# Scores of a linear-attention head in three blocks of 64x64, with sums moved onto TensorE by identity products, and a new written order of the attention stage

## The chip, the cores and the metric

The kernel runs on one core of a Trainium2 chip. The metric is the device time of one execution in microseconds, the median over the runs shown. Engines are named as the profile names them: PE is TensorE's matmul, PEld its weight load, DVE VectorE, ACT ScalarE, POOL GpSimd, SP the queue that issues the transfers.

## The reference

Three stages follow each other. The first is a recurrence with a decaying state for 2 batches of 8 heads (768 steps, 48 wide); its result, 1536 tokens of 384 numbers, goes through two feed-forward layers.

```python
def _attn_ref(r, k, v, w, u) -> np.ndarray:
    ...
    for t in range(S):
        kt, vt, rt, wt = (k[:, :, t], v[:, :, t], r[:, :, t], w[:, :, t])
        cur = np.einsum('bhd,bhe->bhde', u[None] * kt, vt)
        y[:, :, t] = np.einsum('bhd,bhde->bhe', rt, state + cur)
        state = wt[:, :, :, None] * state + np.einsum('bhd,bhe->bhde', kt, vt)

def _moe_ref(x, w_in, w_out) -> np.ndarray:      # 384 -> 2048 -> 384
    h = x @ w_in
    g = np.where(h > 0.0, h, alpha * (np.exp(np.minimum(h, 0.0)) - 1.0))
    return (g @ w_out).astype(np.float32)

def _moe2_ref(x, domain_probs, w1, w2):          # 4 experts, 384 -> 1024 -> 384
    p = domain_probs / (domain_probs.sum(-1, keepdims=True) + 1e-09)
    for e in range(E):
        h = np.maximum(x @ w1[e], 0.0)
        out += p[:, e:e + 1] * (h @ w2[e])
```

## The kernel before

**Attention.** The 768 steps are cut into chunks of 128, six to a batch, so there are 12 chunks, taken in the order SEQ: the two batches alternate, and chunks 0 and 1 of the program are the first of each batch. The 8 heads lie as 4 pairs (p) of two (j): head j of a pair has its 48 rows at partitions 64j to 64j+47. A chunk passes through these steps (name of the token, function, what it does):

- `iw`, `ik`, `lv` load decays, k and r, and v (three buffers each); `su` and `pr` are two scans over the decays on DVE, `kd` and `rd` multiply k and r by them, `g` (own) multiplies r by k.
- `tr` transposes `kd` on PE; `pa` (scores) makes for each head the 128x128 products of its keys and queries; `ow` (own_scores) sums the own products of a step with `ublock`.
- `am` (masked) keeps of the scores what lies above the diagonal, either in one DVE multiplication by `mask` or as an ACT copy and a POOL select.
- `vo` multiplies own scores by v on DVE (tile `bv`); `pp` (update) makes the chunk's part of the state, `us` (updated) adds it to the aged state on DVE, `ws` ages the state.
- `py` (values) sums in two PSUM banks the state's part and the part of the masked scores; `ys` (results) adds both banks to `bv` on DVE; `xs` (parts) splits the sum into a rounded high part and the rest, which the feed-forward products read; `xd` spreads them by a transfer.

**Feed-forward 1.** Its weights come in 32 pieces; `wl` loads one, `wa`, `wb` and `wc` (rest) make its high and low parts. `h` is a hidden block (9 products of 128x128 by 512), `e` and `el` its activation and low part, `z` the second layer (9 products), `dr` takes the sums.

**Order.** Nothing is scheduled: each engine executes its instructions in the order in which the list `ORDER` of such tokens calls the steps; a letter at the end of a token names the engine (A, D, P). A token `n2` adds two products of the tile `idle` (L136) ahead of the next use of a bank: they compute nothing that is used. The first hidden block needs the `x` of four chunks. The list's part up to `|` holds the attention and the first 16 hidden blocks; the experts follow, and there PE runs without a gap.

**Products.** The attention's operands are float32; the profile shows two PE instructions for each such product, and one for each product of the rounded type (fp32r) that the feed-forward layers use. Products whose rows and columns of the array differ (partitions 0 to 63 or 64 to 127 on either side) can stand beside each other.

Of the kernel before, what the change touches and what calls it, by code (L numbers as in the profile page):

```python
# [26 lines left out]
LEAD = 3  # L27
WN = NPAIR * (LEAD + C)
# [46 lines left out]
wl4 wa4D iw1 iw0 su1 ik1 wl0 pr1 ik0 wb4P ik3 kd1P su0 rd1P n2 pa1 tr1A wa0D iw3 pr0 wl2 g1D lv1 rd0D iw5 n2 ow1 kd0P  # L75
n1 pp1 su3 g0D am1S py1 kd3D vo1 wb0P iw2 tr3A lv0 tr0A ik2 g3P pr3 rd3P pa0 lv2 am0S ys1 wl1 lv3 su2 us1 ow0 pp0 py0
pr2 xs1P ws3A wc0P ik4 us0 iw4 vo0 xd1 ow3 wa1D rd2D wa2D lv4 pp3 pa3 am3D wb1P wb2P vo3 n5 py3 su4 ys0 ws2A ys3 wl16
kd2P ik5 wc1P g2P pa2 xs0P lv5 tr2A pr4 ow2 am2M py2 kd4P rd4P iw6 vo2 xd0 wl3 su5 n2 pa4 xs3D ys2 us3 kd5P g4D pp2
pr5 ow4 xs2P ik6 ws5A rd5P am4D g5P us2 xd3 vo4 tr4A wc2P su6 n2 pa5 ow5 vo5 xd2 ws4A iw7 am5M wa16D tr5A wl5 pp4
kd6P wa3D py5 lv6 pr6 py4 wc4P tr6A wb3P ys5 lv7 pp5 rd6D wb16D pa6 wc3P us4 ik7 su7 wl7 us5 wc16P xs5P ws6A am6D h2  # L80
wl17 wa5D iw8 h0 kd7D ys4 e2 wl18 g6P pr7 tr7A ws7A pp6 el2D wb5D h1 wa17D e0 ow6 vo6 us6 ik8 g7P wc5P e1 xd5 wa18D
el0D h3 wb17D rd7P iw9 pp7 wl19 us7 py6 ys6 pa7 wb18P xs6P lv8 el1D wc17D am7M h13 z0 ik9 su8 wa19D ow7 iw11 ws8A
wa7D vo7 xd6 z1 e3 wc18P kd8P py7 tr8A su9 lv9 wl6 wb19P z2 pp8 e13 ys7 wl20 wb7P el3D wc19D pr8 xs7D wl21 rd8D xs4D
wc7D xd7 wl23 h12 wa6D kd9P pa8 z3 g8P e12 wb6P us8 am8D g9D el12D tr9A py8 wc6D xd4 dr3A ow8 wa20D wa21D h15 wb20D
pr9 ik10 vo8 el13P rd9P ws9A lv10 h14 pp9 wl22 e15 ow9 iw10 ys8 wb21D vo9 us9 wa22D pa9 am9D wc20P el15D xs8D h4
wa23D z12 wc21P py9 e14 z13 ik11 su10 wb22P e4 wc22D su11 el14P wb23P kd10P lv11 pr10 h5 el4P rd10P h7 z14 ys9 wc23P
e5 pa10 el5D ws10A am10S h6 kd11P g10D ow10 pr11 vo10 z15 e6 dr15D z4 xs9P py10 g11D xd8 z5 el6D ys10 e7 ow11 rd11D
vo11 pa11 xs10D z6 am11D el7P ws11A py11 ys11 xs11P h16 xd9 e16 h17 xd10 el16P h18 z7 e17 dr7A e18 el17P h19 el18P
z16 xd11 | h8 z17 e19 e8 el8P el19D h9 h10 z18 e9 z8 e10 el9D el10D h11 z9 e11 el11D z10 wl24 wl25 wa25D wa24D h20
z11 wb24P wb25P e20 dr11A z19 h21 wl8 wl10 wc25P dr19D wa8D e21 el20P h22 wl9 wc24P wb8D z20 el21D wa9D e22 wc8P  # L90
wa10D wb9D h23 wl11 z21 wc9P el22D wl26 e23 h24 wb10D wa26D el23D e24 wl12 z22 h25 wc10D wa11D wb26P e25 el24P wb11D
z23 wl14 el25D h28 wc11D wl28 h26 dr23D wa12D wc26D e26 z24 el26D wl27 h27 z25 wb12P e28 wa27D e27 wa28D el28D h29
z26 wb27D el27D wc12P e29 wl29 h31 wc27P wb28D el29D z28 wl13 wa14D e31 wb14P wc28P z27 dr27D h30 wa29D el31P e30
wl15 h32 wa15D z29 el30D wb29P wa13D h35 e32 wc14P el32D z30 wl31 e35 wb13D h33 wa31D wc13P z31 wb15P e33 el35D dr31D
h36 el33P wl30 z32 wa30D h34 wb30P wc29P e36 z33 e34 el34D h37 el36D wc30D h38 wc15D z34 e37 wb31P z36 e38 el38P h39
el37D z35 z37 wc31D dr35D e39 el39P h40 h41 e40 z38 el40P h42 e42 z39 e41 dr39D el41D h43 el42D z40 e43 el43D h44 z41
e44 h45 el44P z42 e45 h46 el45P z43 e46 el46P h47 dr43D z44 e47 z45 z46 el47D z47 dr47D
# [4 lines left out]
def kernel_body(ctx, tc, wkr, vv, uu, w_in, w_out, w1, w2, dp, out):  # L102
# [52 lines left out]
    for t, limit in zip(limits, (1.0, 1 / DOWN)):  # L155
# [106 lines left out]
    def attn(i):  # L262
# [71 lines left out]
        def masked(e):  # L334

            for j in range(2):
                am = tile_of(f"am{j}", 2)
                if e == "D" or (e == "M" and j == 0):
                    mul("D", am, b["pa"][j], mask.unsqueeze(1).to_broadcast([P, NPAIR, C]))
                else:  # L340
                    copy("A", am, b["pa"][j])
                    nc.gpsimd.affine_select(out=am, in_=am, pattern=[[0, NPAIR], [1, C]], compare_op=ALU.is_gt, fill=0.0,
                                            base=0, channel_multiplier=-1)
                free()
# [11 lines left out]
        def update():  # L356
            b["pp"] = pp = bank()[:, :NPAIR * D].rearrange("q (p d) -> q p d", p=NPAIR)
            for p in range(NPAIR):
                for j in range(2):
                    h = 2 * p + j  # L360
                    nc.tensor.matmul(pp[64 * j:64 * j + 64, p, :], lhsT=b["kdt"][:, p, 64 * j:64 * j + 64],
                                     rhs=b["vs"][:, D * h:D * h + D], start=True, stop=True)

        def updated():
            if first:
# [4 lines left out]

        def values():
            b["py"] = py = half_banks()
            if not first:
                for q in range(2):
                    for p, j, o in QUARTERS[q]:
                        nc.tensor.matmul(py[p & 1][64 * o:64 * o + 64, q], lhsT=aged[64 * j:64 * j + D, D * p:D * p + 64],
                                         rhs=b["rd"][64 * j:64 * j + D, p], start=q == 0, stop=False, skip_group_check=True)
# [6 lines left out]
        def results():  # L384
# [4 lines left out]
        def parts(e):  # L389
            split(i, b["bv"], e)  # L390
# [3 lines left out]
                "pp": update, "py": values, "xs": parts, "xd": lambda: spread(i)}  # L394
# [4 lines left out]
    def step(n):  # L399
# [24 lines left out]
        def elu_lo(e):  # L424
            sub(e, b["t"][:, 1], b["e"], b["t"][:, 0])
# [28 lines left out]
    def do(order):  # L454
        for token in order:
# [3 lines left out]
            name, n, e = re.fullmatch(r"([a-z]+)(\d+)([ADMPS]?)", token).groups()  # L459
# [433 lines left out]
def laid_out(i):  # L893
# [17 lines left out]
    vv = np.zeros((P, NCH, 912), np.float32)  # L911
# [3 lines left out]
    vv[:, :, 512:512 + DM] = np.asarray(i["v"]).reshape(2, 8, 6, C, D).transpose(3, 0, 2, 1, 4).reshape(P, NCH, DM)  # L915
    u = np.zeros((2, 64, 4), np.float32)
# [30 lines left out]
```

## Time and profile before

| | |
|---|---|
| median of 3 runs | 650.49 us (650.23 to 650.81) |
| time of the profiled execution | 652.48 us |
| its span, first to last instruction | 650.7 us |
| PE busy | 634.5 us (98%), 3454 instructions |
| DVE busy | 500.2 us (77%), 726 instructions |
| POOL, ACT busy | 358.7 us (55%), 301.8 us (46%) |
| chain of work that ended last | PE 84%, DVE 9%, DMA 3% |

Busy shares are means over the whole span; the stages differ, so the rows below are read by stage. An instruction's own time on PE includes its flight through the array; how fast instructions follow each other is read from the starts of neighbouring groups.

### The profile page before, as it was taken

To read this page: it belongs to the slowest core of one execution; us is meant where nothing else is said; L and a number is where in the kernel's file an instruction comes from. 1 tells how busy PE (TensorE), PEld (TensorE's weight loads), DVE (VectorE), ACT (ScalarE), POOL (GpSimd) and SP (SyncE) were. 2 spreads that over 40 slices of the span, in tenths; PEclk is the share of its full clock that TensorE was granted. 3 is DMA by queue.
4 is the path that set the end of the run, shared out by engine and by line. 5 is a ranking of instruction groups with operands and counts; after the bars stand their busy time and mean duration, and the time that the engine had idled before them with its cause. 6 is when DMAs were issued, how large, how long until landed. Compare 5 with 4: busy or idle time off the path is not lost.

```text
span 650.7 us, 9404 instructions
## 1 busy us (share of the span) xinstructions
PE 634.5 (98%) x3454; PEld 516.1 (79%) x3454; DVE 500.2 (77%) x726; ACT 301.8 (46%) x581; POOL 358.7 (55%) x320
## 2 busy tenths in 40 slices
PE   8898999999999999999999999999999999999995
PEld 6676777788888788888888888888888888888884
DVE  7889998723788854499786886987977968967683
ACT  2437666364766556548353434424443433344230
POOL 5775625231324236546553775876876876854252
PEclk9799999999999999999999999999999999999999
DMA  8747570040322400001212122103121121400012
GB/s 319 246 149 250 186 215 16 13 154 1 95 75 73 131 18 1 0 1 37 103 42 73 34 73 91 25 16 107 41 62 61 42 73 34 123 1 1 0 49 103
DMA packets 20971, 50.94 MB, mean 78 GB/s; under 512 B 2680, under 2 KB 3880, under 8 KB 20916
## 3 DMA queue, kind: packets, MB, share of 16 engines
q1 hardware_dynamic: 20772, 50.25, 23.9%
q8 instruction: 29, 0.48, 0.3%
q14 instruction: 26, 0.21, 0.1%
q10 hardware_dynamic: 144, 0.00, 0.0%
HBM read 46.68 MB, written 2.38 MB: 75 GB/s over the span
## 4 chain that ended last, share of the span: by engine, by line
PE 84%; DVE 9%; DMA 3%; POOL 1%; issue 1%; SPq 0%; ACT 0%; DVEq 0%; POOLq 0%
PE second L666 28%; PE bank L433 13%; PE bank L412 12%; PE chain_a L605 9%; PE chain_b L605 6%; PE chain_p L637 4%; PE chain_c L605 3%; PE chain_d L605 3%; PE chain_e L605 1%; PE bank L323 1%; DMA raw<-in_w_in 1%; DMA kr<-in_wkr 1%; DVE hl L182 1%; DVE raw L219 1%; PE bank L381 1%
## 5 line engine op out<-in xcount | busy, mean ns | idle before, releaser
L666 PE MATMUL second<-hl,w2s 128*128 128x512 f32 x864 | 230.8, 389 | 0.1
L666 PEld LDWEIGHTS second<-hl,w2s 128*128 128x128 f32 x864 | 162.0, 188 | 34.4 <-DVE hl L182 0.5
L684 POOL TENSOR_TENSOR x<-scaled,x 128x512 f32<-128x512 f32 x60 | 84.2, 1424 | 91.5 <-DVE scaled L676 91.3
L412 PE MATMUL bank<-x,w 128*128 128x512 f32 x432 | 105.3, 392 | 0.5 <-DVE e L420 0.5
L433 PE MATMUL bank<-hl,w 128*128 128x512 f32 x432 | 105.1, 391 | 0.0
L659 DVE SCALAR_TENSOR_TENSOR hl<-terms,hl 128x512 fp32r<-128x512 f32 x92 | 96.0, 1055 | 10.6 <-ACT hl L653 10.6
L412 PEld LDWEIGHTS bank<-x,w 128*128 128x128 f32 x432 | 80.3, 188 | 18.4 <-DVE e L420 0.9
L433 PEld LDWEIGHTS bank<-hl,w 128*128 128x128 f32 x432 | 80.5, 188 | 17.6 <-issue 0.7
L182 POOL TENSOR_TENSOR sums<-blocks,sums 128x512 fp32r<-128x512 f32 (+1 forms) x56 | 74.8, 1344 | 28.4 <-ACT sums L186 26.2
L523 POOL TENSOR_TENSOR blocks<-blocks 128x256 f32<-128x256 f32 x84 | 72.6, 883 | 1.1 <-DMA blocks<-in_w 0.4
L420 DVE SCALAR_TENSOR_TENSOR e<-e,bank 128x512 f32<-128x512 f32 x48 | 32.6, 682 | 44.7 <-ACT e L416 43.5
L620 ACT ACTIVATE terms<-chain_b 128x512 f32<-128x512 f32 x28 | 16.7, 598 | 106.0 <-PE chain_b L605 106.0
L653 ACT ACTIVATE hl<-terms 128x512 fp32r<-128x512 f32 x96 | 58.2, 624 | 14.1 <-PE second L666 6.8
L620 ACT ACTIVATE terms<-chain_a 128x512 f32<-128x512 f32 x28 | 16.7, 598 | 77.7 <-PE chain_a L605 77.7
L224 POOL TENSOR_TENSOR raw<-raw,t 128x384 int32<-128x384 int32 x20 | 22.0, 1100 | 51.7 <-ACT t L220 39.3
L605 PE MATMUL chain_a<-x,sums 128*128 128x512 f32 x168 | 47.3, 390 | 0.0
L415 ACT ACTIVATE e<-bank 128x512 f32<-128x512 f32 x48 | 28.4, 593 | 36.8 <-PE bank L412 28.9
L182 POOL TENSOR_TENSOR hl<-e,hl 128x512 fp32r<-128x512 f32 x18 | 23.4, 1297 | 36.6 <-ACT hl L186 36.6
L676 DVE TENSOR_TENSOR scaled<-second,pr 128x512 f32<-128x512 f32 x60 | 40.5, 686 | 3.0 <-PE second L666 1.8
L186 ACT ACTIVATE hl<-e 128x512 fp32r<-128x512 f32 x48 | 30.0, 628 | 24.5 <-DVE e L420 16.7
L617 DVE TENSOR_TENSOR terms<-terms,chain_a 128x512 f32<-128x512 f32 x42 | 28.7, 683 | 14.2 <-PE chain_a L605 13.6
L182 POOL TENSOR_TENSOR w<-raw,w 128x384 fp32r<-128x384 f32 x21 | 22.4, 1070 | 27.6 <-ACT w L186 27.6
(116 smaller groups left out, 1001.0 us busy)
## 6 DMA issues: line engine op xcount, KB each, us to landing
raw<-in_w_in SPq DMA_DIRECT2D x16, 384.0 KB, 3.4
kr<-in_wkr SPq DMA_DIRECT2D x12, 512.0 KB, 6.0
raw<-in_w_out SPq DMA_DIRECT2D x16, 384.0 KB, 3.6
blocks<-in_w SPq DMA_DIRECT2D x16, 384.0 KB, 3.3
raw<-in_w SPq DMA_DIRECT2D x16, 384.0 KB, 4.3
v<-in_vv SPq DMA_DIRECT2D x12, 456.0 KB, 4.7
w<-in_wkr SPq DMA_DIRECT2D x12, 262.5 KB, 4.3
gw<-in_wkr SPq DMA_DIRECT2D x12, 262.0 KB, 2.7
```

What stands on the lines that cost most here:

```text
L182: engines[e].tensor_tensor(o, a, b.bitcast(F32), ALU.subtract)
L412: nc.tensor.matmul(ph, lhsT=wi[:, sa, f, kk, :], rhs=x[:, kk, c0:c0 + nch, sm], start=(kk == 0 and i == 0), stop=(kk == 2 and i == 2))
L420: nc.vector.scalar_tensor_tensor(b["e"], b["e"], -1.0, b["ph"], ALU.add, ALU.max)
L433: nc.tensor.matmul(pxs[q, bl][d][:, :cols], lhsT=wo[:, sa, f, d * P:(d + 1) * P], rhs=b["t"][:, sm], start=(f == 0 and i == 0), stop=(f == ...
L523: nc.gpsimd.tensor_tensor(*(places(blocks[u], p) for p in (r, a, c)), ALU.subtract if op == "-" else ALU.add)
L605: nc.tensor.matmul(banks[c], lhsT=weights(u, r, sa), rhs=tokens(r)[:, sm], start=r in HEADS and i == 0, stop=i == 2, skip_group_check=True)
L620: nc.scalar.activation(out=new({0: 0, 6: 5, 3: 2, 5: 3, 8: 4}[r]), in_=ps, func=AF.Copy, scale=-1.0 if r in (6, 8) else 1.0)
L653: nc.scalar.activation(out=hls[f, b][:, 0], in_=results[f, b], func=AF.Copy if weighted else AF.Relu)
L659: nc.vector.scalar_tensor_tensor(hls[f, b][:, 1], results[f, b], 0.0, hls[f, b][:, 0].bitcast(F32), ALU.max, ALU.subtract)
L666: nc.tensor.matmul(sums[d], lhsT=w[:, sa, f, d * P:(d + 1) * P], rhs=hls[4 * h + f, b][:, sm], start=f == i == 0, stop=f == 3 and i == 2)
L676: nc.vector.tensor_tensor(o, sums[d], prs[h // 2, b], ALU.mult)
L684: nc.gpsimd.tensor_tensor(x2[:, d, s], scaled[d], x2[:, d, s], ALU.add)
```

## The change

Seven edits, all in the attention stage and the weights of feed-forward 1:

1. **Scores** (`pa`): of the four 64x64 blocks of a head's scores the one that the mask clears entirely is no longer made. First keys meet all 128 queries (16 instructions of 64 columns in the array by 128), second keys the last 64 (16 instructions by 64). Neighbouring pairs use opposite halves of the columns. Each head's scores are 384 wide over 4 pairs instead of 512, and `mask` has the same shape, so `am` is always one multiplication of 128x384 for each j.
2. **Values**: the masked part is made in two sets of 16 instructions by 64 columns, second queries over all 128 keys, first queries over 64 keys. For that v is loaded in another layout, 1088 wide instead of 912. The state's part becomes a step of its own, `pq`.
3. **ys with E** (chunks 0 to 4): `bv` is added in PSUM by two products with the identity, in place of two DVE sums.
4. **xs with E** (chunks 0 to 4): ACT copies the high part from PSUM, two products with `minus` (the negated identity) subtract it there, ACT copies the rest out. Before, one ACT copy and one DVE or POOL subtraction.
5. **us with E** (chunks 0 to 3): the aged state is added by an identity product (not for chunks 0 and 1, which have none), and ACT copies the sum.
6. **wc with E** (5 pieces): the low part of a weight piece is made by two products and an ACT copy.
7. **ORDER** is new. Tokens by count up to `|`: `am` 12 on DVE (before 6 on DVE, 3 on both ways, 3 on ACT and POOL), `g` on DVE 1 (6), `rd` on DVE 3 (5), `xs` on DVE 0 (5). Of the `idle` products 11 + 1 are left (13 + 12).

```diff
+wl16 wa16D wl0 iw0 iw1 ik0 wa0D ik1 wl4 su0 wb16P wc16E wb0P kd0P iw2 pr0 rd0P wc0E lv0 su1 pa0 wl17 tr0A wa4D iw5
...
+        def rest(e):
...
+            if e == "E":
+                t = bank()[:, 0:DM]
+                difference(t, hi, wt64[key][:, 0, s])
+                copy("A", lo, t)
+                free()
...
+    def difference(t, a, hi):
+        nc.tensor.matmul(t, lhsT=ident, rhs=a, start=True, stop=False)
+        nc.tensor.matmul(t, lhsT=minus, rhs=hi, start=False, stop=True)
...
         def scores():
-            b["pa"] = pa = [heads_bank() for _ in range(2)]
-            for p in range(NPAIR):
-                for j in range(2):
-                    nc.tensor.matmul(pa[j][:, p, :], lhsT=b["kd"][64 * j:64 * j + D, p, :],
-                                     rhs=b["rd"][64 * j:64 * j + D, p, :], start=True, stop=True)
+            b["pa"] = pa = [bank() for _ in range(2)]
+            for keys in range(2):
+                for q in range(2):
+                    for p in (2 * q, 2 * q + 1):
+                        c = 64 * (keys ^ (p & 1))
+                        for j in range(2):
+                            kd, rd = b["kd"][64 * j:64 * j + D, p, 64 * keys:64 * keys + 64], b["rd"][64 * j:64 * j + D, p]
+                            t = pa[j][c:c + 64, first_block(p).start:384]
...
+                            nc.tensor.matmul(t, lhsT=kd, rhs=rd, start=True, stop=True)
...
-                am = tile_of(f"am{j}", 2)
+                am, pa, wide = tile_of(f"am{j}", 2, (P, 384)), b["pa"][j][:, 0:384], mask.rearrange("q n c -> q (n c)")
...
+        def updated(e):
+            if e == "E":
+                if not first:
+                    nc.tensor.matmul(b["pp"].rearrange("q p d -> q (p d)"), lhsT=ident, rhs=aged[:, 0:NPAIR * D], start=False,
+                                     stop=True, skip_group_check=True)
+                copy("A", state_v, b["pp"])
...
-                    nc.tensor.matmul(py[p & 1][64 * o:64 * o + 64, q], lhsT=b["vs"][:, D * h:D * h + 64], rhs=b[f"am{j}"][:, p],
-                                     start=first and q == 0, stop=True, skip_group_check=True)
+                    nc.tensor.matmul(py[p & 1][64 * o:64 * o + 64, q, 64:128], lhsT=b["vs"][:, D * h:D * h + 64],
+                                     rhs=b[f"am{j}"][:, second_blocks(p)], start=first and q == 0, stop=True, skip_group_check=True)
+            for q in range(2):
+                for p, j, o in QUARTERS[q]:
+                    h, c = 2 * p + j, 64 * (p & 1)
+                    nc.tensor.matmul(py[p & 1][64 * o:64 * o + 64, q, 0:64], lhsT=b["vs"][c:c + 64, D * h:D * h + 64],
+                                     rhs=b[f"am{j}"][c:c + 64, first_block(p)], start=False, stop=True, skip_group_check=True)
...
+        def results(e):
             for m in range(2):
-                nc.vector.tensor_tensor(b["bv"][:, m::2], b["py"][m], b["bv"][:, m::2], ALU.add)
+                if e == "E":
+                    nc.tensor.matmul(b["py"][m], lhsT=ident, rhs=b["bv"][:, m::2], start=False, stop=True, skip_group_check=True)
+                else:
+                    nc.vector.tensor_tensor(b["bv"][:, m::2], b["py"][m], b["bv"][:, m::2], ALU.add)
+                    free()
+
+        def parts(e):
+            if e != "E":
+                split(i, b["bv"], e)
+                return
+            hi, lo = ([x[:, m:4:2, i, s] for m in range(2)] for s in range(2))
+            for m in range(2):
+                copy("A", hi[m], b["py"][m])
+            for m in range(2):
+                nc.tensor.matmul(b["py"][m], lhsT=minus, rhs=hi[m], start=False, stop=True, skip_group_check=True)
+            for m in range(2):
+                copy("A", lo[m], b["py"][m])
                 free()
```

Three places show how the order moves. In these rows a count behind the sizes is that of products (two instructions each for float32), and the line numbers of the change are its own. First, PE from the start of the program, before:

```order
L136 MATMUL bank<-idle 128x256 x13
L323 MATMUL bank<-rd,kd 128x128 x8
L315 MATMUL bank<-ident,kd 128x128 x4
L136 MATMUL bank<-idle 128x256 x2
L331 MATMUL bank<-kr,ublock 64x128 x8
L136 MATMUL bank<-idle 128x256
L361 MATMUL bank<-v,kdt 64x48 x8
```

and in the change:

```order
L138 MATMUL bank<-idle 128x256 x11
L258 MATMUL bank<-raw,ident 128x384
L259 MATMUL bank<-w_124,minus 128x384
L258 MATMUL bank<-raw,ident 128x384
L259 MATMUL bank<-w_131,minus 128x384
L361 MATMUL bank<-rd,kd 64x2x64 x8
L361 MATMUL bank<-rd,kd 64x64 x8
L342 MATMUL bank<-ident,kd 128x128 x4
L138 MATMUL bank<-idle 128x256
```

Two weight pieces' low parts now stand on PE ahead of the first scores, and two of the 13 `idle` products ahead of them are gone.

Second, PE in the middle of the stretch ahead of the first hidden block, where four chunks are under way, before:

```order
L136 MATMUL bank<-idle 128x256 x2
L323 MATMUL bank<-rd,kd 128x128 x8
L361 MATMUL bank<-v,kdt 64x48 x8
L331 MATMUL bank<-kr,ublock 64x128 x8
L315 MATMUL bank<-ident,kd 128x128 x4
L136 MATMUL bank<-idle 128x256 x2
L323 MATMUL bank<-rd,kd 128x128 x8
L331 MATMUL bank<-kr,ublock 64x128 x8
L315 MATMUL bank<-ident,kd 128x128 x4
L361 MATMUL bank<-v,kdt 64x48 x8
L376 MATMUL bank<-rd,sball 64x128 x8
```

and in the change (`sball,ident` is us, `bv,ident` is ys, `x,minus` is xs, `raw,ident` with `w,minus` is wc):

```order
L404 MATMUL bank<-sball,ident 128x192
L440 MATMUL bank<-bv,ident 128x256 x2
L361 MATMUL bank<-rd,kd 64x2x64 x8
L361 MATMUL bank<-rd,kd 64x64 x8
L419 MATMUL bank<-rd,sball 64x128 x8
L453 MATMUL bank<-x,minus 128x256 x2
L342 MATMUL bank<-ident,kd 128x128 x4
L258 MATMUL bank<-raw,ident 128x384
L259 MATMUL bank<-w_131,minus 128x384
L368 MATMUL bank<-kr,ublock 64x128 x8
L397 MATMUL bank<-v,kdt 64x48 x8
```

Where the `idle` products stood, there are now the identity products, between a chunk's own products.

Third, DVE in the same stretch, before:

```order
L179 TENSOR_TENSOR am_614<-bank,mask 128x512
L218 TENSOR_SCALAR t<-raw 128x384
L219 SCALAR_TENSOR_TENSOR raw<-raw,t 128x384
L218 TENSOR_SCALAR t<-raw 128x384
L219 SCALAR_TENSOR_TENSOR raw<-raw,t 128x384
L300 SCALAR_TENSOR_TENSOR a<-w,limits 128x524
L386 TENSOR_TENSOR bv<-bank,bv 128x2x128 x2
L179 TENSOR_TENSOR rd<-kr,a 128x512
L224 ISA raw<-raw,t 128x384x2
L368 TENSOR_TENSOR sball<-sball,bank 128x192
```

and in the change:

```order
L327 SCALAR_TENSOR_TENSOR a<-w,limits 128x524
L185 TENSOR_TENSOR am_546<-bank,mask 128x384
L185 TENSOR_TENSOR am_548<-bank,mask 128x384
L319 SCALAR_TENSOR_TENSOR z<-w,limits 128x524
L321 RECIPROCAL w<-z 128x4
L185 TENSOR_TENSOR bv<-bank,v 128x2x128 x2
L327 SCALAR_TENSOR_TENSOR a<-w,limits 128x524
L319 SCALAR_TENSOR_TENSOR z<-w,limits 128x524
L321 RECIPROCAL w<-z 128x4
L185 TENSOR_TENSOR am_650<-bank,mask 128x384
L185 TENSOR_TENSOR am_652<-bank,mask 128x384
```

The sums with a bank (L386, L368) and the products `rd` have left DVE there, and the scans of the next chunks follow each other more closely.

## Rows read from the trace of the kernel before

**Rows 1.** Busy time by stretch: from:to, length, PE, PEld, DVE, ACT, POOL, clock, DMA.

```profile
0.00:10.60 10.60, 8.89 (x26) 6.97 (x26) 6.76 (x12) 2.80 (x4) 4.67 (x14) 1.00 0.81 282
10.60:54.40 43.80, 37.73 (x516) 29.46 (x516) 38.17 (x68) 18.29 (x44) 31.76 (x30) 0.92 0.68 231
54.40:129.10 74.70, 73.41 (x653) 56.48 (x651) 67.54 (x116) 45.06 (x96) 36.38 (x33) 1.00 0.40 129
200.00:600.00 400.00, 399.45 (x1757) 328.93 (x1756) 313.93 (x420) 180.09 (x340) 248.54 (x217) 1.00 0.16 50
600.00:651.00 51.00, 44.16 (x194) 35.60 (x192) 32.91 (x49) 10.64 (x19) 17.92 (x12) 0.98 0.13 49
```

**Rows 2.** The chain that ended last, 28 to 56 us: start, length, what.

```profile
48.64 1.26 DVE raw L219
...
53.90 1.17 DVE z L292
```

**Rows 3.** PE groups by form, 10.6 to 54.4 us: count, busy, mean ns, idle before.

```profile
L136 PE MATMUL bank<-idle 128*128 128x256 f32 x24 | 7.7, 462 | 0.8 <-DVE am L179 0.8
L361 PE MATMUL bank<-v,kdt 128*64 128x48 f32 x96 | 4.5, 240 | 2.1 <-DVE rd L179 2.1
```

**Rows 4.** PE in order of time: start, length, what, count of instructions.

```profile
12.24 1.03 PE L136 MATMUL bank<-idle 128*128 128x256 f32 x4
...
34.10 1.16 PE L323 MATMUL bank<-rd,kd 48*128 48x128 f32 x16
35.19 0.66 PE L315 MATMUL bank<-ident,kd 128*128 128x128 f32 x4
35.77 0.67 PE L331 MATMUL bank<-kr,ublock 48*64 48x128 f32 x16
36.26 1.02 PE L376 MATMUL bank<-rd,sball 48*64 48x128 f32 x16
...
46.92 0.67 PE L361 MATMUL bank<-v,kdt 128*64 128x48 f32 x16
47.52 0.67 PE L376 MATMUL bank<-rd,sball 48*64 48x128 f32 x16
48.12 1.09 PE L381 MATMUL bank<-am,v 128*64 128x128 f32 x16
49.14 0.67 PE L376 MATMUL bank<-rd,sball 48*64 48x128 f32 x16
...
54.40 4.37 PE L412 MATMUL bank<-x,w 128*128 128x512 f32 x18
```

**Rows 5.** PE in order of time, 45.70 to 45.78 us alone.

```profile
45.73 0.34 PE L331 MATMUL bank<-kr,ublock 48*64 48x128 f32 x4
```

**Rows 6.** Busy time by stretch, around the fall of the clock.

```profile
22.65:24.77 2.12, 0.07 (x4) 0.00 (x0) 1.48 (x4) 0.52 (x1) 0.54 (x1) 1.00 0.55 193
24.77:31.60 6.83, 5.99 (x39) 5.09 (x40) 5.16 (x11) 2.48 (x8) 5.43 (x5) 0.50 0.62 210
```

**Rows 7.** DVE groups by form, 0 to 54.4 us.

```profile
L292 DVE TENSOR_TENSOR_SCAN z<-w,limits 128x524 f32<-128x524 f32 x8 | 9.9, 1233 | 0.0
...
L219 DVE SCALAR_TENSOR_TENSOR raw<-raw,t 128x384 int32<-128x384 int32 x6 | 5.6, 938 | 0.2
L179 DVE TENSOR_TENSOR bv<-bank,v 128x256 f32<-128x256 f32 x12 | 4.5, 415 | 0.9 <-PE bank L331 0.8
L179 DVE TENSOR_TENSOR am<-bank,mask 128x512 f32<-128x512 f32 x6 | 3.9, 676 | 1.6 <-PE bank L323 1.6
L386 DVE TENSOR_TENSOR bv<-bank,bv 128x256 f32<-128x256 f32 x10 | 3.7, 408 | 2.1 <-PE bank L381 2.1
L218 DVE TENSOR_SCALAR t<-raw 128x384 int32<-128x384 int32 x6 | 2.7, 448 | 3.5 <-DMA raw<-in_w_in 3.5
L179 DVE TENSOR_TENSOR kr<-kr 128x512 f32<-128x512 f32 x3 | 2.1, 689 | 0.0
L179 DVE TENSOR_TENSOR rd<-kr,a 128x512 f32<-128x512 f32 x3 | 2.0, 682 | 0.0
...
L368 DVE TENSOR_TENSOR sball<-sball,bank 128x192 f32<-128x192 f32 x3 | 1.0, 342 | 0.0
```

**Rows 8.** ACT in order of time: a copy of 128x256.

```profile
4.49 0.41 ACT L174 ACTIVATE ublock<-u_sb 128x256 f32<-128x256 f32 x1 [1.98 <-DMA u_sb<-in_uu]
```

More of the change, by code (lines that the diff above doesn't have):

```diff
@@ L27 @@
 LEAD = 3
+VN = 1088
 WN = NPAIR * (LEAD + C)
@@ L80 @@
[L80 to L89, printed above, removed]
@@ L166, in kernel_body @@
     make_identity(nc, ident)
-    mask = apool.tile([P, C], F32, name="mask")
+    minus = const.tile([P, P], F32R, name="minus")
+    nc.scalar.activation(out=minus, in_=ident, func=AF.Copy, scale=-1.0)
+    mask = apool.tile([P, 6, 64], F32, name="mask")
     nc.gpsimd.memset(mask, 1.0)
-    nc.gpsimd.affine_select(out=mask, in_=mask, pattern=[[1, C]], compare_op=ALU.is_gt, fill=0.0,
-                            base=0, channel_multiplier=-1)
+    for c in range(2):
+        for part, n in ((mask[64 * c:64 * c + 64, 0:2], 2), (mask[64 * c:64 * c + 64, 3 - c::2], 2)):
+            nc.gpsimd.affine_select(out=part, in_=part, pattern=[[0, n], [1, 64]], compare_op=ALU.is_gt, fill=0.0, base=0,
+                                    channel_multiplier=-1)
     u_sb = const.tile([P, NPAIR, 1], F32, name="u_sb")
@@ L361, in update @@
                     nc.tensor.matmul(pp[64 * j:64 * j + 64, p, :], lhsT=b["kdt"][:, p, 64 * j:64 * j + 64],
-                                     rhs=b["vs"][:, D * h:D * h + D], start=True, stop=True)
-        def updated():
-            if first:
+                                     rhs=b["vo"][:, D * (h // 4 * 2 + j):][:, 0:D] if p & 1 else b["vs"][:, D * h:D * h + D],
+                                     start=p == 0, stop=True, skip_group_check=True)
+        def updated(e):
[4 more added lines that the diff above has]
+                copy("A", state_v, b["pp"])
+            elif first:
                 nc.vector.tensor_copy(state_v, b["pp"])
@@ L369, in updated, with values_of_state @@
             free()
-        def values():
[L372 to L377, printed above, removed]
+        def values_of_state():
+            b["py"] = py = half_banks()
+            for q in range(2):
+                for p, j, o in QUARTERS[q]:
+                    nc.tensor.matmul(py[p & 1][64 * o:64 * o + 64, q], lhsT=aged[64 * j:64 * j + D, D * p:D * p + 64],
+                                     rhs=b["rd"][64 * j:64 * j + D, p], start=q == 0, stop=False, skip_group_check=True)
+        def values():
+            if first:
+                b["py"] = half_banks()
+            py = b["py"]
             for q in range(2):
@@ new lines, in values @@
+            for q in range(2):
+                for p, j, o in QUARTERS[q]:
+                    h, c = 2 * p + j, 64 * (p & 1)
+                    nc.tensor.matmul(py[p & 1][64 * o:64 * o + 64, q, 0:64], lhsT=b["vs"][c:c + 64, D * h:D * h + 64],
+                                     rhs=b[f"am{j}"][c:c + 64, first_block(p)], start=False, stop=True, skip_group_check=True)
+        def results(e):
+            for m in range(2):
+                if e == "E":
+                    nc.tensor.matmul(b["py"][m], lhsT=ident, rhs=b["bv"][:, m::2], start=False, stop=True, skip_group_check=True)
+                else:
+                    nc.vector.tensor_tensor(b["bv"][:, m::2], b["py"][m], b["bv"][:, m::2], ALU.add)
+                    free()
@@ L424, in elu_lo @@
         def elu_lo(e):
-            sub(e, b["t"][:, 1], b["e"], b["t"][:, 0])
+            if e == "E":
+                t = bank()[:, :cols]
+                difference(t, b["e"], b["t"][:, 0])
+                copy("A", b["t"][:, 1], t)
+                free()
+            else:
+                sub(e, b["t"][:, 1], b["e"], b["t"][:, 0])
         def second():
@@ L910, in laid_out @@
     wkr[:, :, KE:] = heads(i["r"]).reshape(P, NCH, 512)
-    vv = np.zeros((P, NCH, 912), np.float32)
+    vv = np.zeros((P, NCH, VN), np.float32)
     v = heads(i["v"]).reshape(2, 64, NCH, NPAIR, C)
```

71 lines of the change are left out of this document (46 added, 25 removed).

## The prediction

> **What bounds the kernel now.** First the busy time by stretch [rows 1]. From 54.4 to 129.1 us PE is busy 73.4 of 74.7 us, from 200 to 600 us 399.45 of 400. At 54.40 the first hidden block of feed-forward 1 starts [rows 4]. From there on the time is PE's work, with 1.3 us of idle to 129.1 and some 7 of idle after 600. So the end is: start of the first hidden block, plus PE's work left behind it, plus this idle.
>
> Ahead of it PE does not set the pace. Of the 43.8 us from 10.6 to 54.4 it is busy 37.7, and 7.7 of these are `idle` products that compute nothing [rows 1, 3]. At warm clock the useful groups there make only 27.5 us (summed below). DVE is busy 6.8 + 38.2 = 44.9 us of the first 54.4 [rows 1]; the chain that ended last runs through it from 48.64 to 53.90 [rows 2], and PE's longest wait there is for DVE's `rd` [rows 3]. DVE's 9.5 us of idle hold 3.5 for the first weights and 6.0 of waits inside the stage, 2.1 of these for the sums `ys` (L386) [rows 7].
>
> So two things are to be counted: PE's work in all, and when the first hidden block can start.
>
> **Cost of one group on PE**, from start to start [rows 4]:
> - Scores, 16 instructions by 128 columns, two beside each other: 34.10 to 35.19, 1.09. Transposes 0.58. Own scores, four beside each other: 0.49 where the state's group follows in the same form (35.77 to 36.26), else as the state's 0.60 (47.52 to 48.12); changing form costs 0.11. Update, by 48 columns, 0.60. Values 1.02 (48.12 to 49.14).
> - New scores: first keys are like own scores, 0.49. Second keys do the same by 64 columns: between half of the 0.44 to 0.49, 0.23, and as much as by 128 columns, 0.44. I take 0.23, because the update's instructions, by 48 columns and only two beside each other, come no slower than 0.60/16 = 0.04 each. With 0.11 for the form: 0.83, a gain of 0.26 a chunk.
> - New values: second queries, two beside each other by 64 columns, as the update, 0.60. First queries, four beside each other, 0.23 (at most 0.44), and 0.15 for one more change of form: 0.98, a gain of 0.04.
> - Four instructions of an identity-like float32 product by 256 took 1.03 us including the flight of the last; I take 0.22 each. So `ys` with E, two products by 256, is 4 x 0.22 = 0.87; `us` by 192, 0.33; `wc` by 384, 0.65 and 0.16 for the rounded part, 0.81; `xs`, two rounded products by 256, 0.22 in all.
>
> The view of a short stretch bears on the second halves: four own-score products started within 0.08 us [rows 5], 0.02 each. The Trainium skill, "TensorE: Matmul & The Clock Gate", section "Wait — 56ns, not 53.3ns?", says that "Start-to-start never drops below ≈25 ns however small N is". By that 16 instructions by 64 would take at least 0.40, nearly my upper bound; the row does not agree with it for products side by side.
>
> **PE's work.** Ahead of the first hidden block, before: 7 scores 7.6, 7 transposes 4.1, 6 own 3.6, 6 updates 3.6, 4 state products 2.4, 6 values 6.1: 27.5. After, by the new order: 7 scores 5.8, 7 transposes 4.1, 6 own 3.6, 6 updates 3.6, 5 state 3.0, 6 values 5.9, 5 `ys` 4.4, 5 `xs` 1.1, 2 `us` 0.7, 5 `wc` 4.1: 36.2. Over the whole kernel PE gets 5 x 0.87 + 5 x 0.22 + 2 x 0.33 + 5 x 0.81 = 10.2 more and 12 x 0.30 = 3.6 less: 6.6 us of added work. All of the added work stands ahead of the first hidden block. Behind it less is left than before: one state product (0.6), 5 scores at 0.26 and 6 values at 0.04 (1.5): 2.0 us less.
>
> So the span becomes 650.7 - (54.4 - S) - 2.0, S being the new start of the first hidden block. Zero gain is S = 56.4.
>
> **S from PE.** The first attention product came at the end of the 10.6 us [rows 1]. Now a second weight piece stands ahead of DVE's first scan (0.45 + 0.94 by its groups [rows 7], less where POOL is quiet), and its load ahead of the first k: I take 1.0 later, 11.6. Two of the `wc` fit ahead of that, in time that `idle` products filled. From 11.6 there are 36.2 - 1.6 + 0.4 (one `idle` product) = 35.0 us of work: S is at least 46.6.
>
> **S from DVE.** Up to the first hidden block it loses 8 `ys` sums (3.3), 4 `us` (1.3), 3 `g` and 3 `rd` (4.1) [rows 7], one `kd`, one `xs`, one scan, two `vo` and one `wb` (some 4.5); it gains two weight pieces (2.8), and 12 `am` of 384 at 0.54 (between 0.342 for 192 and 0.676 for 512 [rows 7]) in place of 6 of 512, 2.5. That is 8 less of 44.9, so 37 of work, which with 3.5 of start is over at 41 without waits. The last bound is now PE's, not DVE's.
>
> **Waits.** Of the 6.0 us of waits on DVE the 2.1 for `ys` go with the sums; 3.9 stay in the loops DVE, POOL, PE, ACT. I add these to PE's bound: S = 46.6 + 3.9 = 50.5.
>
> **What costs nothing, and under what cover.** ACT gets 5 x (4 x 0.41 [rows 8] - 0.6) for `xs`, and small copies for `us` and `wc`, some 8 us; it is busy 18.3 of 43.8 [rows 1]. But PE stands in order behind its copies: between `ys` and `xs` on PE there are two of them (0.8) and mostly a chunk's own scores and update (1.2). Uncovered, a chunk costs about 1 us, 5 in all. POOL takes five `g` and two `rd`, and gives five `wc` and its selects away; it has 12 us free [rows 1]. The v transfers grow by 19% (88 KB, 0.4 us at the stage's 231 GB/s [rows 1]); they are issued a chunk ahead, and would cost 2.3 us for six chunks if they landed late. Nothing of feed-forward 1 behind the first hidden block is slower: DVE was busy 67.5 of 74.7 us there and loses work.
>
> **Sum.** 650.7 - 3.9 - 2.0 = 644.8 for the span, 5.9 less. The profiled execution took 652.48 around its span of 650.7, so it is 2.0 above the median of 650.49 though its span is not; I take the difference on the median: 650.5 - 5.9 = 644.6. Least S, 46.6: 640.7.
>
> **Rivals.**
> - *The second halves don't run four abreast.* 0.21 more for scores and for values, 12 x 0.42 = 5.0: 649.6. For it: no row has a 64-column product four abreast. Against: [rows 5].
> - *The waits stay where they are.* If transfers, POOL and the loops set the stage and not DVE, PE's extra 36.2 - 27.5 = 8.7 us only take the place of the 7.7 us of `idle` products, and S is 54.4 + 1.0 = 55.4: a span of 650.7 + 1.0 - 2.0 = 649.7, a time of 649.5. For it: DVE itself waited 6.0 us.
> - *The clock falls* (the other side). Of 24 `idle` instructions from 10.6 to 54.4 us 2 are left. At 22.65 PE stood still for 2.1 us, and the next 6.83 us ran at half clock [rows 6], 1.2 for 2.4 GHz. Half clock doubles PE's work, and PE is now what bounds the stage. One such stretch costs 3.4 us, so S passes 56.4 from 11.8 us at half clock on; three stretches, 20.5 us, cost 10.2: 654.8. For it: nothing fills a wait any more. Against: 35 of PE's 39 us to S are work, twice as dense as before, and the wait that preceded the fall, for `rd` behind DVE, has its cause removed.
>
> **How the numbers follow.** Forecast 644.6, with a chance of 0.68 (640.7 to 648.5, S from 46.6 to 54.4). The second halves 0.10, the waits 0.10, the clock 0.12. The time is that of the first. The range goes from 640.7 to 650.3, which takes in the two middle rivals with 0.7 us above the later one, and leaves out the clock and a little beside. A measurement of this kernel tells 0.2%, 1.3 us, from no change. Both middle rivals lie within that band, though near its lower edge (649.2), so faster 0.72, same 0.15, slower 0.13.
>
> **What the profile after would show.** First hidden block near 50.5; scores start to start 0.83, values 0.98; PE idle from 11.6 to S under 5 us; granted clock 1.00 throughout; DVE busy near 38 by then, with L386's idle gone. PE busy near 100% behind S as before. The prediction is wrong if S is above 54, which the chain would then show through ACT's copies for `xs` and `wc` or through the loads; or if the second halves take as long as the first.

## The result, and the profile after

The changed kernel takes 643.63 us (median of 4 runs, 642.17 to 644.53), before 650.65: a ratio of 0.9891 (0.9868 to 0.9913), 7.0 us less. The forecast was 644.6. The profiled execution of the change took 642.87 with a span of 641.1, 9.6 less than the 650.7 of the profiled execution before, which was itself 1.8 above the median of its kernel. Two runs are left out of the ratios below as slow: one of the seven of the repetition (709.18 us at a granted clock of 0.845) and one of the twelve with six idle products (654.88 at 0.985).

Busy time by stretch after, with the columns of [rows 1] (PE, PEld, DVE, ACT, POOL):

```profile
0.00:10.80 10.80, 8.39 (x28) 6.24 (x28) 6.41 (x13) 4.98 (x9) 6.64 (x18) 1.00 0.84 298
10.80:49.80 39.00, 37.01 (x762) 28.54 (x762) 35.32 (x59) 23.12 (x66) 30.34 (x27) 1.00 0.90 315
49.80:129.10 79.30, 78.65 (x850) 61.31 (x849) 61.00 (x109) 44.91 (x87) 41.30 (x34) 1.00 0.34 109
```

The stretch ahead of the first hidden block is now 39.0 us instead of 43.8, PE is busy 37.0 of it, and nearly all of that is work; the clock stays at 2.4 GHz where it fell before [rows 6]. Behind it PE is as full as it was.

PE in order of time after, the last 15 us ahead of the first hidden block (L478); L361 scores, L429 and L434 values, L440 ys, L453 xs, L258 and L259 wc, L404 us:

```profile
34.55 0.59 PE L404 MATMUL bank<-sball,ident 128*128 128x192 f32 x2
34.98 1.03 PE L440 MATMUL bank<-bv,ident 128*128 128x256 f32 x4
35.94 0.90 PE L361 MATMUL bank<-rd,kd 48*64 48x128 f32 x32
36.65 0.62 PE L419 MATMUL bank<-rd,sball 48*64 48x128 f32 x16
37.20 0.51 PE L453 MATMUL bank<-x,minus 128*128 128x256 f32 x2
37.55 0.60 PE L342 MATMUL bank<-ident,kd 128*128 128x128 f32 x4
37.99 0.84 PE L258 MATMUL bank<-raw,ident 128*128 128x384 f32 x2
...
40.13 0.90 PE L361 MATMUL bank<-rd,kd 48*64 48x128 f32 x32
40.96 0.69 PE L429 MATMUL bank<-am,v 128*64 128x64 f32 x16
41.58 0.46 PE L434 MATMUL bank<-am,v 64*64 64x64 f32 x16
...
47.27 0.46 PE L434 MATMUL bank<-am,v 64*64 64x64 f32 x16
47.66 0.50 PE L453 MATMUL bank<-x,minus 128*128 128x256 f32 x2
...
49.36 0.66 PE L342 MATMUL bank<-ident,kd 128*128 128x128 f32 x4
49.77 0.48 PE L478 MATMUL bank<-x,w 128*128 128x512 f32 x1
```

Read by the starts: scores 0.83 (40.13 to 40.96), or 0.71 where the state's group of like form follows (35.94 to 36.65); values 0.62 + 0.39; the first hidden block at 49.77, against 54.40 [rows 4].

Where the time went is read from three marks: the start of the first hidden block, the first product of the experts, and the end. The first expert product starts at 279.07 before and at 269.65 after (PE in order of time, one row of each):

```profile
279.07 0.62 PE L637 MATMUL chain_p<-x,sums 128*128 128x512 f32 x2
```

```profile
269.65 0.62 PE L709 MATMUL chain_p<-x,sums 128*128 128x512 f32 x2
```

So 4.6 us came ahead of the first hidden block (54.40 - 49.77) and 4.8 between it and the experts (224.67 - 219.88); the rest, 371.7 before and 371.5 after, differs by 0.2. The 4.8 by kind, each PE instruction counted from its start to the next one's start: scores 5.46 to 3.98, values and state products 10.05 to 8.72 (one chunk's state product fewer), update, own and transposes 7.49 to 6.67, feed-forward products 201.67 to 200.53.

The three longest waits of PE from 10.8 to 49.8 us (us in total, times, longest):

```profile
PE bank L440 <- DVE bv L185: 0.8, 1, 0.8
PE bank L361 <- POOL rd L185: 0.5, 1, 0.5
PE bank L368 <- issue: 0.5, 1, 0.5
```

DVE's `rd`, the longest wait of [rows 3], is gone; nothing is above 0.8 us. The chain that ended last comes from a weight piece's landing through DVE to the first `ys`:

```profile
16.87 0.43 DVE bv L185
...
17.34 1.13 PE bank L440 x4
```

From 17.34 us to the first hidden block it is PE's own work, but for 0.5 us at 42.04 and 1.2 us through ACT at 44.98. So in this execution PE bounds the stretch from 17.34 us on, and DVE sets where that begins.

### The profile page after: what moved, and what is told of

Same layout as the page of the kernel before. It is cut to its first block, busy times and chain, and to the rows that moved or that the text cites. A ratio compares the mean times of both kernels' runs of the same rounds, so it can differ in the third digit from the quotient of the medians.

```text
span 641.1 us, 10200 instructions
## 1 busy us (share of the span) xinstructions
PE 629.7 (98%) x3861; PEld 512.4 (80%) x3861; DVE 481.1 (75%) x706; ACT 303.0 (47%) x589; POOL 362.2 (56%) x321
## 4 chain that ended last, share of the span: by engine, by line
PE 92%; DVE 4%; DMA 1%; issue 1%; ACT 1%; SPq 0%; DVEq 0%; ACTq 0%
PE second L738 28%; PE bank L478 16%; PE bank L505 15%; PE chain_a L677 9%; PE chain_b L677 6%; PE chain_p L709 4%; PE chain_c L677 3%; PE chain_d L677 3%; PE chain_e L677 1%; PE bank L361 1%; DMA raw<-in_w_in 1%; PE bank L368 1%; PE bank L429 1%; PE bank L397 1%; PE bank L419 1%
## 5 line engine op out<-in xcount | busy, mean ns | idle before, releaser
L478 PE MATMUL bank<-x,w 128*128 128x512 f32 x432 | 106.2, 392 | 0.6 <-DVE e L486 0.6
L478 PEld LDWEIGHTS bank<-x,w 128*128 128x128 f32 x432 | 80.3, 188 | 18.1 <-ACT w L192 1.1
L188 POOL TENSOR_TENSOR hl<-e,hl 128x512 fp32r<-128x512 f32 x24 | 31.3, 1305 | 58.4 <-ACT hl L192 54.8
L230 POOL TENSOR_TENSOR raw<-raw,t 128x384 int32<-128x384 int32 x23 | 25.0, 1092 | 38.0 <-ACT t L226 29.6
L677 PEld LDWEIGHTS chain_a<-x,sums 128*128 128x128 f32 x168 | 31.5, 188 | 6.9 <-DVE terms L689 0.4
```

The source lines that it names most:

```text
L188: engines[e].tensor_tensor(o, a, b.bitcast(F32), ALU.subtract)
L478: nc.tensor.matmul(ph, lhsT=wi[:, sa, f, kk, :], rhs=x[:, kk, c0:c0 + nch, sm], start=(kk == 0 and i == 0), stop=(kk == 2 and i == 2))
L677: nc.tensor.matmul(banks[c], lhsT=weights(u, r, sa), rhs=tokens(r)[:, sm], start=r in HEADS and i == 0, stop=i == 2, skip_group_check=True)
```

## The experiments

Below, S is the start of the first hidden block in the one profiled execution of each kernel, "half" the time ahead of S that its trace gives PE's clock at half, and "first ys" the start of chunk 0's identity products, where the new order has them. The ratios are to the kernel before, of runs on one chip.

| kernel | ratio (interval) | S | half | first ys |
|---|---|---|---|---|
| before | 1 | 54.40 | 6.8 | |
| the change | 0.9891 (0.9868 to 0.9913) | 49.77 | 0 | 17.34 |
| full scores, new order, sums | 0.9941 (0.9923 to 0.9959) | 52.72 | 0 | 19.85 |
| blocks, new order, no sums | 1.0078 (1.0056 to 1.0100) | 61.64 | 34.1 | |
| new order alone | 1.0105 (1.0081 to 1.0129) | 61.08 | 27.3 | |
| sums alone, old order | 1.0121 (1.0097 to 1.0146) | 60.25 | 0 | |
| only the low parts (wc) back | 0.9950 (0.9927 to 0.9974) | 54.66 | 10.2 | 20.84 |
| only ys, xs, us back | 1.0036 (1.0019 to 1.0053) | 59.71 | 20.5 | |
| no sums, 36 idle products | 1.0091 (1.0070 to 1.0112) | 60.19 | 6.8 | |
| three wc in POOL's waits | 0.9897 (0.9878 to 0.9915) | 51.56 | 0 | 19.34 |
| the change again | 0.9902 (0.9879 to 0.9924) | 55.29 | 10.2 | 19.76 |
| six idle products added | 0.9947 (0.9918 to 0.9975) | 51.61 | 0 | 17.46 |
| earlier scan | 0.9896 (0.9872 to 0.9920) | 49.40 | 0 | 17.00 |
| earlier scan, three wc | 0.9900 (0.9871 to 0.9929) | 50.61 | 3.4 | 17.04 |

S is one execution's, while a ratio is that of several runs: the unaltered kernel alone has S at 49.77 and at 55.29.

**Full scores.** The diff of the change in `scores`, `masked`, `values`, `mask` and v undone, the rest kept:

```diff
-                            nc.tensor.matmul(t, lhsT=kd, rhs=rd, start=True, stop=True)
+            for p in range(NPAIR):
+                for j in range(2):
+                    nc.tensor.matmul(pa[j][:, p, :], lhsT=b["kd"][64 * j:64 * j + D, p, :],
+                                     rhs=b["rd"][64 * j:64 * j + D, p, :], start=True, stop=True)
```

> The changed kernel (643.6) with its new order and its sums on TensorE, but with the scores, the mask and the values of before: all four 64x64 blocks of a head, values in one set of 16 instructions by 128, v in the old layout, masking 512 wide. Theory: the blocks are worth 0.26 us of PE a chunk in the scores and little in the values, and 0.13 us of DVE for each masking. Scores start to start 1.09 again; the first hidden block 1.8 to 3 us later than the 49.8 of the changed kernel, and 1.4 to 2 us more of PE behind it: 646.5 to 648.5. Rival: the second set of value products and the changes of form eat what the blocks save, and the whole gain is from sums and order: 643 to 644.5.

Measured 647.75. PE in order of time in this kernel (L348 scores, L408 the state's product):

```profile
39.21 1.16 PE L348 MATMUL bank<-rd,kd 48*128 48x128 f32 x16
40.30 0.67 PE L408 MATMUL bank<-rd,sball 48*64 48x128 f32 x16
```

The scores take 1.09 again. From S to the experts it is 221.57 instead of 219.88, 1.7 more, of which the scores are 1.48 (5.46 against 3.98). S is 2.95 later, but 2.5 of this is the later first `ys` (19.85 against 17.34), which the unaltered kernel shows too in its second profile; from there to S the two differ by 0.4. The time is as the theory had it, the blocks are worth about half a per cent (0.9941 against 0.9891 and, again, 0.9902), and 1.7 us of this is shown behind S; what they give ahead of S this one trace does not settle. The values give next to nothing behind S, 6.04 against 5.94.

**No sums.** In `ORDER` every E is replaced: us and ys by D, xs and wc by P.

> The changed kernel with its new order and its blocks, but every sum that it moved to TensorE back on the engine it came from: ys and us on DVE, xs and the five weight pieces' low parts on POOL. Theory: PE loses 10 us of work ahead of the first hidden block, which it does not need; DVE gets some 5 us and POOL some 12 us, and POOL, 33 of the first 50 us busy in the changed kernel, becomes late. First hidden block at 53 to 56, time 647 to 650. Rival: the order alone lets it start early and the sums only fill PE: first hidden block at 50 or before, time 640 to 643.5.

Measured 655.91, later than either the theory or the rival. The chain that ended last, 28 to 38 us (start, length, what):

```profile
28.40 1.27 POOL x L188
...
34.37 1.13 POOL w L188
35.51 1.47 POOL rd L185
```

It goes through POOL as the theory said, which does the subtractions (`x`, `w`) there, and POOL is busy 10.00 of the 10 us from 30 to 40. But the clock stood at half for 34.1 us of this execution too, which the expectation did not count.

**Order alone.** Both edits above together: new order, no blocks, no sums.

> The kernel before with nothing but the new order: full scores and values, no sums on TensorE (ys and us on DVE, xs and the five low parts on POOL; masking always on DVE; the state's product as a step of its own). Theory: the order was made for engines that are relieved and gives nothing without the sums: DVE has 12 maskings of 512 and all sums, POOL its 12 us more. First hidden block at 55 to 58, time 650 to 654. Rival: the order is most of the gain: 645 to 648.

Measured 658.00, above the theory's upper end, far from the rival; the clock stood at half for 27.3 us here, which the theory did not count either. Behind S this kernel needs 222.66 to the experts, 2.0 less than before with the very same products (a state product moved ahead is 0.6 of it): the order alone shortens that stretch, and lengthens the one ahead.

**Sums alone.** The old order with E on us, ys, xs of the first chunks and wc of pieces 0 to 4, full scores; xs stands directly behind ys.

> The kernel before with its old order and full scores, but with the sums on TensorE: ys and xs of chunks 0 to 4, us of chunks 0 to 3, the low parts of weight pieces 0 to 4 (xs directly behind ys, since banks do not suffice otherwise). The idle products stay. Theory: DVE is relieved by 5 us and POOL by some 10 us, PE has the 10 us, of which the waits hold 8; the first hidden block at 51 to 54, and PE's work behind it as before: 647 to 650. Rival: the identity products and ACT's copies stand in PE's way in an order not made for them: 652 to 658.

Measured 658.95: the rival. The clock did not fall ahead of S; the longest waits from 10 to 60 us are:

```profile
POOL am L367 <- ACT am L190: 16.4, 4, 9.3
ACT x L190 <- PE bank L424: 8.8, 2, 4.9
DVE am L183 <- PE bank L348: 8.2, 2, 6.4
```

In the old order ACT also copies scores for masking (`am`). There ACT waits for the identity products (L424 is ys), POOL for ACT's copies, and DVE for scores that stand on PE behind all this. So neither order nor sums give anything alone; each alone costs 1.0 to 1.2%. Together they give 0.6%, and with the blocks 1.1%.

**Which sums.** The wc alone, and ys, xs and us alone, put back in the same way.

> The changed kernel with only the five weight pieces' low parts (wc 16, 0, 17, 4, 3) back on POOL, in the places where they stand; ys, xs and us stay on TensorE. Theory: POOL sets the pace when the sums go back (in the run without any sums the chain went through POOL); it gets 5 x 1.1 = 5.5 us, two of them ahead of the first kd, and PE loses 4.1 us that it could use. First hidden block at 51.5 to 54 instead of 49.8, time 645.5 to 648.5. Rival: PE bounds the stretch, as the prediction had it, and what leaves PE comes out of the time: first hidden block at 46 to 48, time 640 to 642.

> The changed kernel with ys and us of the first chunks back on DVE and xs on POOL; the five low parts stay on TensorE. Theory: DVE gets 5.4 us and POOL 6.5; first hidden block at 53 to 57, time 647 to 651, and with fewer products on PE the clock falls for some stretch. Rival: the low parts were all that mattered: 643 to 645.

Measured 647.60, within its theory, and 653.29, above it (S too, 59.71). Both sets count, the second more (1.0036 against 0.9950), but with different times at half clock, 10.2 and 20.5 us, so the two prices are not those of the sums alone. S of the first, 54.66, lies above the expected band: its first `ys` starts 3.5 us later than that of the change, and its ten quickest runs alone reach from 644.33 at a mean clock of 0.997 to 650.73 at 0.989.

**The clock or POOL.** The kernel without sums, with 36 idle products that compute nothing:

```diff
-... pa1 ... ow1 ...
+... n4 pa1 ... n2 ow1 ...
```

> The changed kernel without any of the sums on TensorE (655.9 when run as such, first hidden block 61.6, clock at half for 33 us), with 36 idle products added that compute nothing: four ahead of each of six chunks' scores and two ahead of each of six own scores. Theory A, the clock: PE at half clock makes the loops longer, and with the clock held at 2.4 GHz the first hidden block comes 4 to 7 us earlier, time 649 to 652. Theory B, POOL alone: its work sets the pace whatever the clock, first hidden block at 60 to 63, time 654.5 to 657.

Measured 656.79, and the clock at half for 6.8 us instead of 34.1. The chain of this kernel, 35 to 44 us:

```profile
35.63 1.47 POOL rd L185
...
37.15 0.90 PE bank L361 x32
...
42.08 1.93 PE bank L138 x8
```

POOL's `rd` ends at 37.10 and releases the scores, in the kernel without the idle products at 36.98 with the clock at half: up to there POOL sets the pace whatever the clock, and time and S are theory B's. Behind it the idle products (L138) stand on the chain themselves, so what the clock costs after 37 us is not settled by this run.

**Room on PE, from both sides.** Three wc moved to where POOL waits; and six idle products added.

```diff
-... ow2 wc17E ... ws3A wc4E ... tr4A wc3E ...
+... rd3P wc17P wc4P ... wb1P wc3P ...
```

> The changed kernel with three of the low parts (17, 4, 3) on POOL, but in places where the trace shows POOL waiting (2.9 us for k of chunk 4, 3.5 us for a scan); 16 and 0 stay on TensorE. PE loses 2.6 us of work ahead of the first hidden block. Theory (PE bounds the stretch once POOL and DVE are free of the sums): first hidden block at 47.5 to 48.8, time 641 to 642.6. Rival (the scan of chunk 5 on DVE, which ended at 45.1, sets it by way of rd and the scores): 49.5 to 50, time as the change, 643 to 644.

> The changed kernel with six idle products (2.6 us of PE work that computes nothing) ahead of the scores and own scores of chunks 2, 3 and 4. Theory A (PE bounds the stretch ahead of the first hidden block): the first hidden block and the end come 2.0 to 2.6 us later than in the unaltered kernel. Theory B (the loops through DVE, ACT and POOL bound it, and PE has room): 0 to 0.8 us later.

2.6 us less work on PE gave 0.9897 (644.43, near the rival), the same as the change. 2.6 us more gave 0.9947 (646.68) where the unaltered kernel beside it had 0.9902: 2.9 us by the ratios, but the intervals touch, and two of its runs, at mean clocks of 0.986 and 0.988, took 653.05 and 653.64. The traces say more if S is read from the first `ys` on. With six idle products the stretch from there to S takes 34.2 us, in the change 32.4, so 1.7 us of the 2.6 come out, nearer to theory A. With three wc fewer it takes 32.2, though PE has 2.6 us less to do; that its S is later than the change's is the later first `ys`. Its chain that ended last is PE's from 19.34 us on, but leaves PE here and comes back at 31.20:

```profile
23.86 0.06 DVE am L185
...
30.64 0.43 DVE bv L185
```

So PE bounds the stretch when it gets more. When it gets less, DVE, with two scans and two weight pieces from 23.86 to 31.07 us, takes its place: another bound lies right beside it.

**Again, and the scan earlier.** The unaltered kernel beside two with three tokens moved:

```diff
-... wa17D vo0 ... wa1D wa2D ... am6D ... pr5 ...
+... vo0 wa17D ... wa1D pr5 ... am6D wa2D ...
```

> The changed kernel once more, unaltered, beside the others on one chip: 642 to 645, as in its first four runs, and the comparison for the three that follow. Theory A says that the start of the first hidden block, 49.8 in its first profile, is set by PE's own work and so repeats within 0.5 us; theory B, that the loops between the engines set it, lets it move by 1 us or more from one execution to the next, as transfers land a little earlier or later.

> The changed kernel with three tokens of the order moved: vo0 ahead of wa17D (the first identity product of ys waited 0.75 us for it), pr5 directly behind wa1D, and wa2D behind am6D, so that the scan of chunk 5 and the state's sum come some 2.5 us earlier on DVE. Theory A: PE's work stays, only its waits of some 2.5 us shrink: 0.5 to 1.2 us faster than the unaltered kernel. Theory B: the loops get shorter: 1 to 2 us faster. Rival: other waits take their place, within 0.4 us.

> The same three tokens moved, and the three low parts (17, 4, 3) on POOL in its waits, which by themselves gave nothing (644.4). Theory A: with DVE's steps earlier, PE's 2.6 us less of work now show: 2 to 3 us faster than the unaltered kernel. Theory B: as the kernel with the tokens alone, and no faster than it by more than 0.5 us.

Ratios of 0.9902, 0.9896 and 0.9900: no difference. These moves don't improve the order of the change, and there is no kernel here that beats it. What the repetition showed is how S moves. Its profiled execution had S at 55.29, 5.5 later than the first one of the same program. DVE, POOL and PE in order of time, in the first profile of the change:

```profile
10.64 0.36 DVE L224 TENSOR_SCALAR t<-raw 128x384 int32<-128x384 int32 x1 [0.54 <-DMA raw<-in_w_in]
10.75 1.30 POOL L185 TENSOR_TENSOR kd<-kr,z 128x512 f32<-128x512 f32 x1
11.04 1.43 DVE L225 SCALAR_TENSOR_TENSOR raw<-raw,t 128x384 int32<-128x384 int32 x1
12.39 1.23 DVE L327 TENSOR_TENSOR_SCAN a<-w,limits 128x524 f32<-128x524 f32 x1
...
17.34 1.13 PE L440 MATMUL bank<-bv,ident 128*128 128x256 f32 x4 [0.75 <-DVE bv L185]
```

and in the repetition:

```profile
11.09 1.20 POOL L185 TENSOR_TENSOR kd<-kr,z 128x512 f32<-128x512 f32 x1
11.25 1.25 DVE L224 TENSOR_SCALAR t<-raw 128x384 int32<-128x384 int32 x1 [1.05 <-DMA raw<-in_w_in]
12.53 1.51 DVE L225 SCALAR_TENSOR_TENSOR raw<-raw,t 128x384 int32<-128x384 int32 x1
13.96 1.23 DVE L327 TENSOR_TENSOR_SCAN a<-w,limits 128x524 f32<-128x524 f32 x1
...
19.76 1.43 PE L440 MATMUL bank<-bv,ident 128*128 128x256 f32 x4 [1.85 <-DVE bv L185]
```

A weight piece landed 0.6 us later. In the first profile DVE began on it 0.11 us ahead of POOL's `kd`, and its first operation took 0.36 us; here it began 0.16 behind `kd` and took 1.25, and the scan came 1.6 later. The other traces go the same two ways: of the seven with the same work up to there, the four in which DVE began first (the change, six idle, both earlier scans) have 0.36 or 0.37 us and the first `ys` at 17.0 to 17.5, the three in which POOL began first (again, full scores, three wc) 1.12 to 1.25 us and the first `ys` at 19.3 to 19.9. Why the operation takes longer then, no run here shows. Busy time by stretch of the repetition:

```profile
10.00:20.00 10.00, 7.13 (x143) 5.03 (x142) 8.83 (x13) 3.96 (x9) 7.29 (x6) 1.00 1.01 387
20.00:30.00 10.00, 10.00 (x123) 7.27 (x122) 7.16 (x12) 3.65 (x13) 6.22 (x6) 0.52 0.79 272
```

PE waited 1.9 us for `bv` instead of 0.8, did 7.1 us of work in the 10 us instead of 8.5, and ran at half clock from 20.5 to 30.7: 123 instructions from 20 to 30 us where the first profile has 199. So the 5.5 us are 2.4 by which the first `ys` came later (19.76 against 17.34), plus 4.4 by which the products from there to chunk 2's transposes (L342) took longer, mostly at half clock (19.76 to 30.56, 10.8 us, against 17.34 to 23.71, 6.4), less 1.3 by which the rest of the way to S was shorter.

## Why the prediction was right, step by step

- **The end is S plus PE's work behind it.** Right: over the expert part the two traces differ by 0.2 us, and behind S PE stands idle for 0.7 us up to the experts.
- **S = 50.5.** Measured 49.77, but by three terms that were off and nearly cancel, which is luck. The first attention product started at 10.84 us and not at 11.6. PE's work from there was taken as 35.0 and was 37.0; the waits as 3.9 and were 2.0 (37.0 of 39.0 busy). The identity products were undersized: ys 0.96 (34.98 to 35.94) for 0.87, xs 0.35 for 0.22, us 0.43 for 0.33, wc 0.94 (37.99 to 38.93) for 0.81, and more beside other forms, 11.1 us up to S in all for the 8.6 of the sum. Transposes, 0.44 for 0.58, gave some back.
- **Scores 0.83 and the second halves.** Right, 0.83 and less beside a like form; the rival that they run no faster than the first halves fell. By the Trainium skill's page "TensorE: Matmul & The Clock Gate", section "Wait — 56ns, not 53.3ns?", starts never lie closer than about 25 ns; 16 products of the second halves would by that take at least 0.40 and the scores about 1.0, an estimate from the page's figure. The trace shows 0.83, and 32 instructions in 0.71, 0.022 each, beside a like form, so the measurement decides. Values came to 1.01 for 0.98, no gain over 1.02.
- **Behind S 2.0 us less.** This is the term that was mis-sized: it was 4.8 (the parts as I gave them make 2.1). Scores gave 1.5 for 1.3, the values 0.2 as counted, and the state's products 1.1 for 0.6. Put at nothing were update, own scores and transposes, which gave 0.8, and the feed-forward products, 1.1. The new order alone is 2.0 shorter there than before: in it one state product has moved ahead, and groups of like form stand together (own scores take 0.44 ahead of the state's product, transposes 0.41 ahead of a hidden block). The 1.1 are PE's waits in that stretch, 1.8 us before and 0.7 after. With the order alone they are still 1.7, and 0.6 to 0.7 with the order and either the sums or the blocks.
- **The profile's own time.** The sum was made against 650.7, and its 5.9 was taken off the median. The traces gained 9.6, the medians 7.0: the profiled execution of before was slower than its median, that of the change faster. That the forecast of the time is off by 1.0 us only, and that of the span by 3.7, is luck. Of the 3.7 us by which the span was missed, 2.8 are the mis-sized term and 0.7 is S.
- **The bound moves from DVE to PE.** Right for the profile of the change, whose chain is PE's from 17.34 us on, and six idle products bear it out; but three wc taken away show that nothing is gained below it. DVE's work was undersized: it was busy 41.7 us up to S (6.4 + 35.3), where the prediction had 37; with three wc fewer on PE the chain goes through DVE for 7 us, so DVE is the near bound. POOL, which the prediction gave 12 us of room, is the bound where the sums are put back: without the sums on PE the chain goes through POOL's subtractions. The prediction counted that POOL is relieved of five wc, but not of its xs, and gave neither a part in S. How much POOL's relief weighs against DVE's is not shown.
- **The clock rival.** It was given the wrong place: it does not decide the median, but it is in the change. One of its two profiled executions had S at 55.29, above the 54 from which the prediction called itself wrong; of the signs that it named, the loads have a part (the weight piece), ACT's copies none. Its price was about right: 10.2 us at half clock make 5.1 by it, and the products in that stretch took 4.4 longer. That the work on PE, denser than before (35 of 39 us against 27.5 of 43.8, which is not twice), protects the clock was right for the first profile only.

## What to carry to other kernels

Where one engine sets the pace and another burns its waits with empty products, let the second do the first one's sums, even at a poor rate: here some 13 us of identity products on TensorE, with the blocks and an order written for them, brought the first hidden block 4.6 us forward; the same sums in the old order cost 1.2%. Count a group of small products with its neighbours: what it costs depends on whether the next one has the same form. When a stretch is balanced to within 2 us between engines, little decides it: in one execution here a transfer that landed 0.6 us later went with a start 5.5 us later. So time it in many runs before judging a change of half a per cent, and read where a shift of S begins before giving it to the edit.

## What the hardware showed that I had not expected

- The clock fell to half without any pause of PE above 1.9 us (in the repetition), and did not fall in a kernel with the same 1.9 us wait (three wc).
- The time from PE's last product to the end of the span was 6.2 us in one execution of the change and 8.4 in the other, 6.5 before and 8.7 with full scores (the span less the end of PE's last product, as 641.1 - 634.9 for the first). With S, this is what differs between the two profiled executions of one program.
- Two DVE operations on a weight piece, 128x384 of integers, took 0.36 and 0.56 us at their quickest (26.91 and 27.30 us of the change, POOL idle) and up to 1.25 and 1.51 while POOL worked (the repetition). POOL at work does not alone make them slow: the 0.36 at 10.64 us of the change lies beside POOL's `rd` and the start of its `kd`.
